# Where the small work stands in an attention and MLP block: splits, heads' pieces, the last steps and two sums

## The chip, the cores and the metric

The kernel runs on one core of a Trainium2 chip. The metric is the device time of one execution in microseconds, lower is better; several executions are timed and their median is taken. Engines are named as the profile names them: PE (matrix products; PEld its weight loads), DVE, ACT, POOL, and SP, which here issues every DMA. Each engine works through its instructions in the order in which the program lists them, and waits where an input isn't there yet.

## The reference

One transformer block with adaptive layer norm, 2048 tokens of width 512, 32 heads of width 16, an MLP of width 1792 with mish, all in float32.

```python
mod = (_silu(c) @ w_mod).reshape(c.shape[0], 6, 1, -1)
sa, ca, ga, sb, cb, gb = (mod[:, 0], mod[:, 1], mod[:, 2], mod[:, 3], mod[:, 4], mod[:, 5])
h = _layernorm(x, axis=-1) * (1 + ca) + sa
x = x + ga * _A_ref(h, A_wqkv, A_wo)          # softmax attention over all heads
h = _layernorm(x, axis=-1) * (1 + cb) + sb
x = x + gb * _B_ref(h, B_w1, B_b1, B_w2)      # up (1792) + mish + down (512)
return x
```

where the attention's part is

```python
scores = jnp.einsum("bhqd,bhkd->bhqk", q, k) * scale
p = _softmax(scores, axis=-1)
o = jnp.einsum("bhqk,bhkd->bhqd", p, v)
```

and mish(h) = h tanh(log(1 + e^h)).

## The kernel before

**Steps.** The attention runs over 4 blocks of 512 queries, here called quarters (`qb`), with 8 groups of 4 heads in each (`g`; `n` counts the 32 groups through), and 16 chunks of 128 keys in each group. That makes T = 512 steps `t` of one chunk for one group. A step multiplies scores for its chunk (`score`, L507, four products that use one half of PE's rows), turns them to exponentials on ACT (L515), and adds the weighted values of two steps earlier (`pv`, L535, eight records in the profile). PRO = 20 steps ahead of the scores, the maxima of the scores of later groups are computed (`max_tile`, product L471, reduction on DVE L473). A group's negated maxima are put in place once a group (`max_rows`, L487 to L496: a transpose, two DVE operations, four DMAs `qa<-mt`), in the fourth step before the group begins; the product of the scores subtracts them. In the last 20 steps there are no maxima left to compute.

**Half-steps and hooks.** Everything else is hung between these products. `at(h, f)` lists the function f to be called at half-step h; step t calls the hooks of 2t at its start and those of 2t+1 in its middle. Hooks of one half-step run in the order in which they were listed. A quarter has 256 half-steps, a group 32. `step` writes the order out: what a hook issues is queued on its engine behind all that was issued earlier.

**Units beside the attention.** `queue` holds units: projections of q, k and v in the first quarter, and afterwards, for the query block that the attention has finished, the output projection (`wo_unit`), 14 up units (`up_unit(f)`, 12 products) and 20 down units (`down_unit`, 6 or 12 products). `next_part`, called every second step, cuts the next piece of a unit: all of its products if there are 8 or fewer left, else half of them, so 6 of 12. Each product of a piece is done in two halves, over the lower and over the upper 64 rows (`mm_half`), one in each of the two steps, beside a score or a maximum's product that takes the other half of the rows. A piece of k products gives k halves to each of two steps. Each half is followed by a product of the attention; the first half of the next step waits for the exponential (or the reduction) that reads the product issued right behind the last half (`after`), because both halves add up in one bank. In the last 20 steps a step with f halves spreads its four scores over f slots; with no halves it does two scores at a time.

**Mish.** When an up unit f ends at half-step h (`fin`), its mish is hung at offsets from h, one stage each: clamp (POOL, L735), exponential (ACT, L741), product (POOL, two operations, L749 and L750), logarithm (ACT, L753), inverse (ACT, L756), quotient (POOL, five operations, L765 to L769), place (no instruction), split (POOL, L95 writes `a_h`, L98 writes `a_l`). `done["a", f]` says when a down unit that reads f may begin. In the last part (`idle(h)`) the bias is added on DVE rather than on ACT. While f = 0 to 4 an up unit ends every 8 half-steps; from f = 5 on a down unit stands between, and it is 12 (later 16).

**Heads.** When a group's weighted sums are complete, `evac` copies them to `ot` and hangs up, from `2 * t1`, two half-steps behind the boundary of the group: `sums` (a DMA of the denominators), `rows` (four DMAs `od<-ot`, L564), the reciprocal and its way to `rb`. Every second group, three POOL operations multiply by `rb` (L579) and split the result into `o_hl` (L95, L98). `od` is one buffer for two groups: the rows of the next pair may be written only when the last of these three has read it.

**Modulation and weights.** In the first quarter the other eight half rows of `w_mod` are loaded (`mod_load`), multiplied and added up on POOL (`sums`, L618 to L620), and summed over the partitions by PE (`mod_unit`). These are `specials`: `do_specials` runs at most one a step, at its end; later the same queue holds the transposes of the normed rows. Each modulation sum starts the load of the one two places on; the last one starts `start_preps`, which splits all the weights of the MLP and the output projection (32 `prep_unit`s) and writes them back to HBM.

**The end.** The last query block has no attention left to stand beside. `tail_loads`, at half-step 2T - 30, loads weights for it: `wos`, and `w1s` for f = 0 to 3. Of these f = 2 and 3 go to the two buffers that also serve the last up units. `tail` then does the output projection of this block, the ten down units that were held back (`held`), the layer norm and the MLP. Between the last step and `tail` a loop runs what is still hung up.

Of the kernel before, what the change touches and what calls it, by code (L numbers as in the profile page):

```python
# [18 lines left out]
def adaln_block(ctx: ExitStack, tc: tile.TileContext, x, wqkv, wo, w1, b1, w2, c, w_mod, out):  # L19
# [9 lines left out]
    NB = S // TB  # L29
# [3 lines left out]
    T = 16 * NIT  # L33
# [5 lines left out]
    PRO = 16 + LEAD  # L39
# [46 lines left out]
    def dap(t, off, ap):  # L86
        return bass.AP(tensor=t.tensor, offset=t.offset + off, ap=ap)

    def hi_copy(eng, hi, src):
        if eng == "a":  # L90
            nc.scalar.copy(hi, src)
        elif eng == "v":
            nc.vector.tensor_copy(hi, src)
        else:
            nc.gpsimd.tensor_scalar(hi, src, 1.0, 0.0, op0=ALU.mult, op1=ALU.add)  # L95

    def lo_sub(eng, lo, src, hi):
        (nc.gpsimd if eng == "p" else nc.vector).tensor_sub(lo, src, hi.bitcast(F32))  # L98
# [25 lines left out]
    def mm_go(m):  # L124
        acc, l, r, start, stop = m
        nc.tensor.matmul(acc, l, r, start=start, stop=stop)  # L126
# [11 lines left out]
    def pe_run():  # L138
        while pe_queue:
            mm_go(pe_queue.pop(0))  # L140
# [13 lines left out]
    def bank(tag="ms"):  # L154
        return ring() if tag == "ring" else ps.tile([P, TB], F32, tag=tag, name="bk", bufs=1)
# [29 lines left out]
    def at(h, f):  # L185

        hooks.setdefault(h, []).append(f)
# [122 lines left out]
    with ExitStack() as es:  # L310
# [107 lines left out]
        for tb in range(NB):  # L418
# [5 lines left out]
            for kind in (1, 0) if tb == 0 else (1,):  # L424
                fin = qk_unit(kind, 0, tb, "ring")
# [117 lines left out]
    def evac(n):  # L543
        qb, g = divmod(n, G)
        t1 = 16 * (n + 1) + 1
        if g == 0:
            o_hl[qb] = [ap.tile([P, DK, TB], F32R, tag=f"o_{i}", name="o_hl", bufs=1) for i in range(2)]
        ot = ap.tile([P, TB], F32, tag="ot", name="ot", bufs=1)
        nc.scalar.copy(ot, accs.pop(n))
        if g % 2 == 0:  # L550
            st["od"] = ap.tile([P, TB], F32, tag="od", name="od", bufs=1)
            st["rb"] = ap.tile([P, TB], F32, tag="rb", name="rb", bufs=1)
        od, rb = st["od"], st["rb"]
        b = 64 * (g % 2)
        if n == NIT - 1:
            mst["last"] = (ot, od, rb)
            return
        sm = ap.tile([P, 16], F32, tag="sm", name="sm", bufs=2)
        def sums():
            nc.sync.dma_start(sm, ot[DH::32, :])  # L560

        def rows():
            for h in range(4):
                nc.sync.dma_start(od[b + 16 * h:b + 16 * h + 16, :], ot[32 * h:32 * h + DH, :])  # L564

        rc = ap.tile([P, 16], F32, tag="rc", name="rc", bufs=2)
        hurry = g == G - 1
        at(2 * t1 + 2, sums)
        at(2 * t1 + (12 if g == 2 else 3), rows)
        at(2 * t1 + (5 if hurry else 12), lambda: nc.vector.reciprocal(rc, sm))  # L570
        at(2 * t1 + (6 if hurry else 13), lambda: nc.sync.dma_start(rscr[n], rc))
        at(2 * t1 + (8 if hurry else 17),
           lambda: nc.sync.dma_start(rb[b:b + 64, :], dap(rscr, n * 4 * TB, [[TB, 4], [0, DH], [1, TB]])))
        if g % 2 == 1 or n == NIT - 2:
            r = slice(0, P if g % 2 else 64)

            oh, ol = o_hl[qb]
            k, d = 2 * t1 + (36 if g == 1 else 11 if hurry else 23), 0 if hurry else 2
            at(k, lambda: nc.gpsimd.tensor_mul(od[r], od[r], rb[r]))  # L579
            at(k + d, lambda: hi_copy("p", oh[r, g // 2, :], od[r]))  # L580
            at(k + 2 * d, lambda: lo_sub("p", ol[r, g // 2, :], od[r], oh[r, g // 2, :]))
# [85 lines left out]
    def load_w1(f):  # L667
        return load_split("w1", 2, w1scr[f])
# [42 lines left out]
    def up_mms(acc, w, hh, hl):  # L711
        mm3(acc, [w1v(w, 0, k) for k in range(DK)], [w1v(w, 1, k) for k in range(DK)],
            [hh[:, k, :] for k in range(DK)], [hl[:, k, :] for k in range(DK)], "b")
# [67 lines left out]
    def idle(h):  # L781

        return h is not None and 2 * (T - PRO) + 2 < h <= 2 * T
# [5 lines left out]
    def block(qb, t0):  # L789

        xn, y, act, w1s, w2s, wos, done, hx = {}, {}, {}, {}, {}, {}, {}, []
# [58 lines left out]
        def up_unit(f, tag):  # L850
            w = w1s.pop(f)
            acc = bank(tag)
            up_mms(acc, w, *hx)
            act[f], (bias, *stages) = mish(f, acc, False)

            def fin(h):
                bias(idle(h))
                for i, s in zip((1, 3, 4, 9, 13, 13 if f < 4 else 14, 16, 18) if f < 5 else (1, 5, 6, 9, 13, 14, 16, 18), stages):
                    at(h + i, s)
                done["a", f] = h + 20  # L860
                if f + 2 < FT:
                    w1s[f + 2] = load_w1(f + 2)
                elif qb + 1 < len(blocks):
                    blocks[qb + 1]["w1"][f + 2 - FT] = load_w1(f + 2 - FT)
            return fin
# [95 lines left out]
    def half_tile(t, j, scr):  # L961

        w = t[:, j * 2 * D:(j + 1) * 2 * D]
        nc.sync.dma_start(w.bitcast(F32), scr.rearrange("p v m -> p (v m)"))
        return w.rearrange("p (v m) -> p v m", v=2)

    def w1_tail(f):
        i, j = divmod(f % 8, 2)
        return load_w1(f) if i == 1 else half_tile(ka[(1, 0, 2, 3)[i]], j, w1scr[f])

    def tail_loads():
        for k in range(DK):
            wos[k] = half_tile(ka[(4, 0)[k // 2]], k % 2, woscr[k])
        for f in range(4):
            w1s[f] = w1_tail(f)

    def tail():
# [4 lines left out]
        for i in range(4):  # L982
            r = 4 * last + i
            nc.sync.dma_start(y[i], x[r * P:(r + 1) * P, :])
        for f in range(4, 8):
            w1s[f] = w1_tail(f)
        accs4 = [bank("ms"), bank("acc")] + [None, None]

# [51 lines left out]
        act, stages = {}, {}  # L1040
        LAG = 4
        for u in range(FT + LAG):
# [11 lines left out]
            f = u - LAG  # L1054
            if f >= 0:
                a_h, a_l = act.pop(f)
                w = w2s.pop(f)
                for i in range(4):
                    s = slice(i * P, (i + 1) * P)
# [14 lines left out]
    units, specials = [], []  # L1074
# [9 lines left out]
    def next_part(h):  # L1084

        if not cur["left"] and units and h >= units[0][0]():
            cur["h"] = h
            cur["fin"] = units.pop(0)[1]("ms")
            cur["left"], cur["first"] = list(pe_queue), True
            cur.pop("after", None)  # L1090
            pe_queue.clear()
        slots = []
        for m in cur["left"]:
            if slots and len(slots[-1]) < 2 and m[0].shape[-1] <= TB // 2:
                slots[-1].append(m)
            else:
                slots.append([m])
        n = len(slots)
        k = n if n <= 8 else (n + 1) // 2
        cur["part"], cur["left"] = slots[:k], [m for l in slots[k:] for m in l]  # L1100

    def whole_units(h, credit):
# [24 lines left out]
    def step(t):  # L1127
# [23 lines left out]
        if not second and 1 < t < T:  # L1151
            next_part(2 * t)
# [67 lines left out]
            f()  # L1220

    def do_specials(h):
        if specials and h >= specials[0][0]():
            fin = specials.pop(0)[1]()
            pe_run()
            at(h + 1, lambda: fin(h + 1))


    plan = [(-PRO, 2, 0, range(4, 16)), (-PRO, 1, 1, range(NB)), (-PRO, 0, 1, (0,)), (-PRO, 1, 2, range(NB)),
# [128 lines left out]
```

## Time and profile before

| what | us |
|---|---|
| runs: median (lowest, highest) | 1726.91 (1724.11, 1729.96) |
| the profiled execution | 1725.0 |
| its span | 1723.2 |
| busy: PE / DVE / ACT / POOL | 1677.6 / 1427.8 / 1341.0 / 887.3 |
| L471, products for maxima, 2048 | 782.1 |
| L507, products for scores, 2048 | 719.9 |
| L535, weighted sums, 4096 records | 547.2 |
| L473, reductions on DVE, 2048 | 1278.4 |
| L515, exponentials on ACT, 2048 | 1089.0 |

In a row of a timeline the first number is the start in us from the start of the span, the second the duration (of all that the row merges; x4 means four instructions), then engine, line, operation, what it writes <- what it reads, and the shape; in brackets, if the engine was idle before it, for how long and what ended that. A row of the waits has the waiting engine and line, what it waited for, and us in total, the number of waits, the longest. Matmuls overlap on PE, so their durations add up to more than the time; the distance between starts is what counts.

### The profile page before, as it was taken

Reading aid. Unit: us, or ns where it says so; the run is one execution under the profiler, and the core shown is the slowest. Engines: PE = TensorE matmul, PEld = TensorE weight load, DVE = VectorE, ACT = ScalarE, POOL = GpSimd, SP = SyncE. Lnnn points to the kernel's source line nnn. Section 1 sums busy time; section 2 is a strip of 40 time slices with the busy share of each in tenths; the row PEclk is TensorE's granted clock in tenths of the full one; section 3 lists DMA queues with packets and bytes.
Section 4 is the critical chain, followed back from the end, with each engine's and each line's share of the span. In section 5 each row is a group of like instructions: output and inputs, shape, how many; then the busy total and the mean of one; then the engine's idle time right before and its main releaser. Section 6 shows DMA issues by size and latency. Waiting matters only on the chain.

```text
span 1723.2 us, 32800 instructions
## 1 busy us (share of the span) xinstructions
PE 1677.6 (97%) x12236; PEld 930.9 (54%) x12236; DVE 1427.8 (83%) x2352; ACT 1341.0 (78%) x2605; POOL 887.3 (51%) x868
## 2 busy tenths in 40 slices
PE   7999999999999999999999999999999999999998
PEld 5755655455435454555555554555555545553676
DVE  6888888888898888888888888888888888880467
ACT  6257777777779898888889898888888888888364
POOL 5155224565403297755524496655433687636542
PEclk9999999999999999999999999999999999999999
DMA  7677456777763333435342644344343534332261
GB/s 239 186 226 220 113 175 196 241 231 218 224 201 86 104 101 84 119 77 154 101 111 64 195 104 101 92 130 117 97 110 97 163 82 115 92 105 105 98 228 65
DMA packets 113993, 240.03 MB, mean 139 GB/s; under 512 B 24049, under 2 KB 49649, under 8 KB 107785
## 3 DMA queue, kind: packets, MB, share of 16 engines
q1 hardware_dynamic: 113832, 237.92, 48.8%
q8 instruction: 97, 1.59, 0.4%
q14 instruction: 64, 0.52, 0.1%
HBM read 179.95 MB, written 51.44 MB: 134 GB/s over the span
## 4 chain that ended last, share of the span: by engine, by line
PE 82%; POOL 6%; DMA 5%; ACT 3%; DVE 2%; issue 1%; SPq 1%; ACTq 0%; DVEq 0%; POOLq 0%
PE bk L535 26%; PE ring L471 21%; PE ring L507 19%; PE bk L132 8%; PE bk L126 3%; PE ring L126 2%; ACT pr L515 2%; DMA qscr<-ql 1%; PE ring L1061 1%; DMA w2scr<-hl 1%; POOL y L880 1%; POOL a_l L98 1%; DMA ka<-kscr 1%; DMA wma<-in_w_mod 1%; DVE mx L473 1%
## 5 line engine op out<-in xcount | busy, mean ns | idle before, releaser
L473 DVE TENSOR_REDUCE mx<-ring 128x1 f32<-128x512 f32 x2048 | 1278.4, 684 | 180.3 <-PE bk L132 122.6
L515 ACT ACTIVATE pr<-ring 128x512 f32<-128x512 f32 x2048 | 1089.0, 611 | 235.4 <-PE bk L132 153.1
L471 PE MATMUL ring<-ka,qa 64*128 64x512 f32 x2048 | 782.1, 427 | 8.3 <-ACT pr L515 7.4
L507 PE MATMUL ring<-qa,ka 64*128 64x512 f32 x2048 | 719.9, 398 | 11.5 <-DMA qa<-mt 6.8
L471 PEld LDWEIGHTS ring<-ka,qa 64*128 64x128 f32 x2048 | 366.9, 184 | 421.8 <-DVE mx L473 355.3
L535 PE MATMUL bk<-pr,vg 128*32 128x512 f32 x4096 | 547.2, 606 | 0.0
L507 PEld LDWEIGHTS ring<-qa,ka 64*128 64x128 f32 x2048 | 373.4, 185 | 115.6 <-ACT pr L515 47.8
L132 PE MATMUL bk<-h,w 64*128 64x512 f32 x1008 | 283.1, 412 | 1.5 <-ACT pr L515 1.5
L132 PE MATMUL bk<-w,a_h 64*128 64x512 f32 x576 | 194.0, 416 | 0.5 <-ACT pr L515 0.5
L132 PEld LDWEIGHTS bk<-h,w 64*128 64x128 f32 x1008 | 172.5, 185 | 11.2 <-ACT pr L515 4.4
L535 PEld LDWEIGHTS bk<-pr,vg 128*32 128x32 f32 x4096 | 81.2, 108 | 126.2 <-issue 118.7
L735 POOL TENSOR_SCALAR ee<-hb 128x512 f32<-128x512 f32 x42 | 62.4, 1486 | 102.5 <-ACT hb L729 100.5
L765 POOL TENSOR_TENSOR ee<-ee,rr 128x512 f32<-128x512 f32 x42 | 53.8, 1280 | 117.0 <-ACT rr L756 116.8
L132 PE MATMUL bk<-w,a_l 64*128 64x512 f32 x288 | 113.5, 394 | 0.0
L132 PEld LDWEIGHTS bk<-w,a_h 64*128 64x128 f32 x576 | 95.6, 185 | 9.2 <-ACT pr L515 3.3
L880 POOL TENSOR_TENSOR y<-yd,y 128x512 f32<-128x512 f32 x50 | 64.2, 1284 | 45.9 <-ACT yd L879 44.9
L132 PE MATMUL bk<-w,o_hl 64*128 64x512 f32 x288 | 79.6, 409 | 0.0
L98 POOL TENSOR_TENSOR a_l<-hb,a_h 128x512 fp32r<-128x512 f32 x53 | 71.7, 1352 | 4.4
L753 ACT ACTIVATE rr<-ee,two 128x512 f32<-128x512 f32 x56 | 40.6, 726 | 21.4 <-POOL ee L750 12.7
L132 PE MATMUL bk<-h_h,wl 64*128 64x512 f32 x168 | 57.0, 422 | 0.0
L750 POOL TENSOR_TENSOR ee<-ee,rr 128x512 f32<-128x512 f32 x42 | 54.1, 1288 | 3.5
L769 POOL TENSOR_TENSOR hb<-hb,rr 128x512 f32<-128x512 f32 x42 | 54.2, 1289 | 3.3
(204 smaller groups left out, 1805.5 us busy)
## 6 DMA issues: line engine op xcount, KB each, us to landing
ka<-kscr SPq DMA_DIRECT2D x124, 384.0 KB
w<-w2scr SPq DMA_DIRECT2D x56, 512.0 KB
w<-w1scr SPq DMA_DIRECT2D x46, 512.0 KB
vg<-vscr SPq DMA_DIRECT2D x32, 552.0 KB
qa<-qscr SPq DMA_DIRECT2D x124, 100.0 KB
kscr<-qh SPq DMA_DIRECT2D x16, 512.0 KB
qscr<-qh SPq DMA_DIRECT2D x32, 256.0 KB
hl<-in_B_w SPq DMA_DIRECT2D x28, 256.0 KB
```

Source lines behind the costliest of these rows:

```text
L98: (nc.gpsimd if eng == "p" else nc.vector).tensor_sub(lo, src, hi.bitcast(F32))
L126: nc.tensor.matmul(acc, l, r, start=start, stop=stop)
L132: i = nc.tensor.matmul(acc, l[64 * g:64 * g + 64], r[64 * g:64 * g + 64], start=start, stop=stop)
L471: nc.tensor.matmul(pm, qt[64 * s:64 * s + 64, qs * P:(qs + 1) * P], kt[64 * s:64 * s + 64, kb * TB:(kb + 1) * TB], start=True, stop=True)
L473: return nc.vector.tensor_reduce(out=mxs[n][:, s, 4 * j + qs, kb:kb + 1], in_=pm, op=ALU.max, axis=AX.X)
L507: nc.tensor.matmul(p_, kt[64 * s:64 * s + 64, kc * P:(kc + 1) * P], qt[64 * s:64 * s + 64, :], start=True, stop=True)
L515: e = nc.scalar.activation(pr, p_, AF.Exp, scale=SCALE)
L535: nc.tensor.matmul(accs[n][32 * h:32 * h + 32, :], vgs[n][:, o:o + 32], pts.pop((t, h)), start=(kc == 0), stop=(kc == 15))
L735: nc.gpsimd.tensor_scalar_min(buf("ee", 2), b["hb"], HCAP)
L750: nc.gpsimd.tensor_mul(ee, ee, rr)
L769: nc.gpsimd.tensor_mul(hb, hb, rr)
L880: nc.gpsimd.tensor_add(y[i], yd, y[i])
```

## The change

Four things.

- In `up_unit` the stages of f = 4 and later keep their places but for the split, which goes from 18 to 19, and `done` from 20 to 21 (`late`). For f = 4 the quotient was at 14 already.
- In `evac` the three POOL operations of a quarter's second group (g = 1) go from 36, 38, 40 to 42, 46, 50; for the other groups but the last of a quarter the distance between them goes from 2 to 4. The rows of the third group (g = 2) go from 12 to 24.
- In `next_part` a piece has 3 products from half-step 2(T - PRO) on, that is in the last 20 steps; `tail_loads` loads two blocks of w1 instead of four, and `tail` the others.
- `do_specials` may run two in a step in the first quarter.

```diff
-        at(2 * t1 + (12 if g == 2 else 3), rows)
+        at(2 * t1 + (24 if g == 2 else 3), rows)
...
-            k, d = 2 * t1 + (36 if g == 1 else 11 if hurry else 23), 0 if hurry else 2
+            k, d = 2 * t1 + (42 if g == 1 else 11 if hurry else 23), 0 if hurry else 4
             at(k, lambda: nc.gpsimd.tensor_mul(od[r], od[r], rb[r]))
             at(k + d, lambda: hi_copy("p", oh[r, g // 2, :], od[r]))
             at(k + 2 * d, lambda: lo_sub("p", ol[r, g // 2, :], od[r], oh[r, g // 2, :]))
...
-                for i, s in zip((1, 3, 4, 9, 13, 13 if f < 4 else 14, 16, 18) if f < 5 else (1, 5, 6, 9, 13, 14, 16, 18), stages):
+                late = f >= 4
+                for i, s in zip((1, 3 if f < 5 else 5, 4 if f < 5 else 6, 9, 13, 13 + late, 16, 18 + late), stages):
                     at(h + i, s)
-                done["a", f] = h + 20
+                done["a", f] = h + 20 + late
...
     def tail_loads():
         for k in range(DK):
             wos[k] = half_tile(ka[(4, 0)[k // 2]], k % 2, woscr[k])
-        for f in range(4):
+        for f in range(2):
             w1s[f] = w1_tail(f)
...
-        for f in range(4, 8):
+        for f in range(2, 8):
             w1s[f] = w1_tail(f)
...
         k = n if n <= 8 else (n + 1) // 2
+        if h >= 2 * (T - PRO):
+            k = 3
...
     def do_specials(h):
-        if specials and h >= specials[0][0]():
-            fin = specials.pop(0)[1]()
-            pe_run()
-            at(h + 1, lambda: fin(h + 1))
+        for _ in range(2 if h < 2 * T // NB else 1):
+            if specials and h >= specials[0][0]():
+                fin = specials.pop(0)[1]()
+                pe_run()
+                at(h + 1, lambda fin=fin: fin(h + 1))
```

## The prediction

> **What bounds the kernel now.** I read the chain that ended last first, then the weighted sums (PE line L535, eight records a step) as a ruler for the length of a step, then the stretches where a step is long.
>
> ```profile
> PE 82%; POOL 6%; DMA 5%; ACT 3%; DVE 2%; issue 1%; SPq 1%; ACTq 0%; DVEq 0%; POOLq 0%
> ```
>
> The chain is PE's for 82%, but POOL, which is busy only half the time, holds 6%. A plain step takes 2.84 us (first row below, from one L535 to the next). The other rows, in time order, are the stretches that matter: a long step in each of the last three quarters, what follows the second and third of them, and a slightly long one; the columns are the stretch's length, busy us (and instructions) of PE, PEld, DVE, ACT and POOL, the granted clock, the DMA share and GB/s.
>
> ```profile
> 658.65:661.49 2.84, 2.84 (x25) 1.55 (x23) 2.78 (x6) 1.58 (x4) 2.76 (x4) 1.00 0.13 53
> 661.49:667.35 5.86, 3.38 (x25) 1.54 (x23) 3.27 (x7) 3.26 (x7) 2.39 (x3) 1.00 0.01 3
> ...
> 1035.12:1041.89 6.77, 4.32 (x25) 1.96 (x23) 3.46 (x7) 3.69 (x7) 2.36 (x3) 0.84 0.01 2
> 1041.89:1045.34 3.45, 3.45 (x26) 1.60 (x24) 2.33 (x5) 2.43 (x6) 1.48 (x1) 0.82 0.46 152
> 1410.22:1416.80 6.58, 4.11 (x25) 1.79 (x23) 3.42 (x8) 3.57 (x7) 2.47 (x3) 0.88 0.01 2
> 1416.80:1420.50 3.70, 3.70 (x24) 1.58 (x22) 2.37 (x5) 2.47 (x5) 1.48 (x1) 0.76 0.42 146
> ...
> 681.49:684.65 3.16, 3.16 (x24) 1.46 (x22) 2.67 (x6) 3.11 (x7) 0.02 (x1) 1.00 0.21 44
> ```
>
> The three long steps sit at the same place of their quarter: at the mish of up unit f=5, 8 steps after the heads' pieces of the quarter's second group. The timelines of PE, ACT and POOL show who waits for whom.
>
> ```profile
> 662.49 0.28 PE L487 MATMUL ring<-ident,mm 128*32 128x128 f32 x1
> 665.25 0.50 PE L471 MATMUL ring<-ka,qa 64*128 64x512 f32 x1 [2.48 <-ACT pr L515]
> ...
> 664.00 0.72 ACT L753 ACTIVATE rr<-ee,two 128x512 f32<-128x512 f32 x1 [2.98 <-POOL ee L750]
> ...
> 635.06 1.29 POOL L579 TENSOR_TENSOR od<-od,rb 128x512 f32<-128x512 f32 x1
> ...
> 647.97 1.31 POOL L98 TENSOR_TENSOR o_hl<-od,o_hl 128x512 fp32r<-128x512 f32 x1
> ...
> 660.04 0.62 POOL L95 TENSOR_SCALAR a_h<-hb 128x512 fp32r<-128x512 f32 x1
> 660.75 1.29 POOL L98 TENSOR_TENSOR a_l<-hb,a_h 128x512 fp32r<-128x512 f32 x1
> 662.00 0.62 POOL L749 TENSOR_SCALAR rr<-ee 128x512 f32<-128x512 f32 x1
> 662.70 1.26 POOL L750 TENSOR_TENSOR ee<-ee,rr 128x512 f32<-128x512 f32 x1
> 668.02 1.49 POOL L735 TENSOR_SCALAR ee<-hb 128x512 f32<-128x512 f32 x1 [4.05 <-ACT hb L729]
> ```
>
> POOL has run without a gap since before 635 and is some 5 us late; f=5's product (L749, L750) ends at 663.96; ACT's logarithm waits 2.98 us for it, with the exponentials of the scores queued behind it on ACT; PE then has no score bank left and waits 2.48 us. Right behind, POOL is idle for 4.05 us: the jam is one of order, not of load.
>
> **The split behind the next product (`late`).** For f=4 the split goes from 18 to 19 half-steps behind its unit, f=5's product stays at 6, and the two units end 12 apart (half-steps 356 and 368 in the second quarter): 374 against 374 before (the split was registered first), 375 against 374 after. So a_h and a_l change places with the product. From 660.04 to 662.00 that is 1.96 us, and the product ends at 662.00. ACT then waits 1.0 instead of 2.98, PE about 0.5 instead of 2.48. Nobody waits soon for the split itself: the down units that read f=4 are queued some 30 half-steps later, and its `done` moves by one with it. **Gain 3 x 1.95 = 5.9 us.** At least 0 (if POOL fills the time otherwise), at most the whole waits, 3 x 2.5 = 7.5.
>
> **The clock behind two of the stalls.** In the second and third stall the granted clock falls to 0.82 and 0.76 over the following step. Against the first stall's 5.86 and a plain 2.84, they cost 0.91 + 0.61 and 0.72 + 0.86 more, **3.1 us** together. With stalls of 0.5 us I take all of it as gone; it stays if an equal gap stays (bounds 0 and 3.1). The Trainium skill ("TensorE: Matmul & The Clock Gate", HAM oscillation) warns only of idle gaps over about 3.4 us; by that rule a gap of 2.5 us would not lower the clock, this term would be 0 and the time 1715. Here the rows speak for the gap: the low clock comes right behind it both times, and the other rows show 1.00.
>
> The same order matters for f=6 and f=7, where a small wait shows:
>
> ```profile
> 681.54 0.72 ACT L753 ACTIVATE rr<-ee,two 128x512 f32<-128x512 f32 x1 [0.49 <-POOL ee L750]
> ...
> ACT rr L753 <- POOL ee L750: 12.7, 12, 3.0
> ```
>
> Three of the twelve waits are the 3.0s; the rest is small. A step with one is 3.16 long, 0.32 over a plain one, and I count two such steps in each of three quarters: **1.9 us**, gone when the product stands 1.96 us earlier (bounds 0 and 1.9).
>
> **The heads' pieces further apart.** For the second group the three POOL operations move from 358, 360, 362 to 364, 368, 372: still ahead of f=5's product at 374, so the same 3.2 us stand before it. With POOL never idle there, their order among themselves moves nothing: each operation's input (the yd copy, ACT's exponential and inverse, rb) is there before POOL comes to it. **0**; if POOL did run dry in between, up to 1 us of loss a quarter. For other groups the spread is 4 more half-steps on a POOL that has gaps: 0. The rows' DMA of the third group goes from 14 to 26 half-steps behind the boundary of its group, one half-step ahead of the negated maxima's DMAs on SP. That queue is in order:
>
> ```profile
> 649.30 2.98 SPq L564 DMA_DIRECT2D od<-ot  x4
> ...
> 663.48 2.81 SPq L496 DMA_DIRECT2D qa<-mt  x4
> ...
> SPq L496 <- DVE mx L473: 194.3, 18, 15.7
> ```
>
> Today the rows wait until 649.27 for the heads' last subtraction (od is read until then). Moved, that subtraction ends at about 660.0, the four DMAs take 2.98 us and are issued by 663.0, while the maxima are not there before 663.46: **0**, by half a microsecond; if SP is 3 us later than that, PE waits (rival (e)).
>
> **Three halves a step at the end.** In the last 20 steps no maxima run. Now the first ten take six halves each and the last ten none.
>
> ```profile
> 1549.80:1578.31 28.51, 26.47 (x182) 12.01 (x182) 3.42 (x7) 23.14 (x46) 16.47 (x16) 1.00 0.34 130
> 1578.31:1598.69 20.38, 20.38 (x121) 6.48 (x120) 1.00 (x2) 19.87 (x43) 14.03 (x13) 1.00 0.15 40
> ...
> 1573.88 0.38 PE L132 MATMUL bk<-h,w 64*128 64x512 f32 x1
> 1574.10 0.40 PE L132 MATMUL bk<-h,w 64*128 64x512 f32 x1
> ...
> 1576.71 0.50 PE L132 MATMUL bk<-h,w 64*128 64x512 f32 x1 [0.51 <-ACT pr L515]
> ...
> 1578.31 1.07 PE L535 MATMUL bk<-pr,vg 128*32 128x512 f32 x8
> ...
> 1579.96 1.06 PE L535 MATMUL bk<-pr,vg 128*32 128x512 f32 x8
> ...
> 1575.06 0.63 ACT L756 ACTIVATE rr<-rr 128x512 f32<-128x512 f32 x1
> 1575.58 1.08 ACT L515 ACTIVATE pr<-ring 128x512 f32<-128x512 f32 x2
> ...
> 1593.90 7.25 ACT L515 ACTIVATE pr<-ring 128x512 f32<-128x512 f32 x14
> ```
>
> 48.9 us in all. In the first part ACT is busy 23.1 of 28.5 us, and yet PE waits for it: the first half of a step waits for the exponential of the score beside the last half of the step before (`after`), here the one that ends at 1576.66. So any further ACT operation lengthens a step. In the second part ACT is busy throughout. A step of two slots takes 1.65 (1578.31 to 1579.96), and pairs start 0.22 to 0.23 us apart, so six slots make 2.57 and four (four scores, three with a half beside them) 2.12. PE's slots are 80 before and 80 after; what is to be gained is overlap with ACT. ACT has 80 exponentials of 0.518 (7.25 over 14), 2.07 a step, and five other operations instead of eight, since f=13's three fall behind the end, each 0.52 (1575.06 to 1575.58) to 0.6. The halves now wait for the third exponential of a step, not the fourth, so for 0.52 less than with six slots, and PE's own 2.12 decides. 20 x 2.14 + 5 x 0.55 = 45.6, **3.3 less**. The last exponentials lag a little less. I take **3.5**; bounds: ACT alone, 80 x 0.518 + 2.75 = 44.2, gains 4.7; steps as long as with six slots, 20 x 2.57, lose 2.5.
>
> f=13's mish now runs behind the last weighted sum, where POOL was idle until the tail's layer norm:
>
> ```profile
> 1602.28 0.59 ACT L549 COPY ot<-bk 128x512 f32<-128x512 f32 x1 [1.14 <-PE bk L535]
> ...
> 1615.34 0.19 POOL L106 TENSOR_SCALAR ln_rs<-ln_mv 128x1 f32<-128x1 f32 x1 [11.09 <-DVE ln_mv L105]
> ...
> 1575.83 1.28 POOL L765 TENSOR_TENSOR ee<-ee,rr 128x512 f32<-128x512 f32 x1 [7.04 <-ACT rr L756]
> ...
> 1584.13 1.28 POOL L98 TENSOR_TENSOR a_l<-hb,a_h 128x512 fp32r<-128x512 f32 x1
> ```
>
> Behind the copy at 1602.87 come the exponential (0.62), the product (1.96), logarithm and inverse (1.35), then quotient and split, 1575.83 to 1585.41 less a clamp between them (1.49, row at 668.02), 8.1: 12 us and some handing over, to about 1615, just as the layer norm asks for POOL. **A loss of 0.5**, between 0 and 2. SP is freed of a long wait by `range(2)`; what waited behind it has slack, 0, and the two later loads are needed only some 45 us on.
>
> **Two sums in one step.**
>
> ```profile
> 124.84 0.72 POOL L620 TENSOR_TENSOR wm<-wm 128x256 f32<-128x256 f32 x1
> ...
> 124.47 0.67 PE L126 MATMUL ring<-wm,ones 128*128 128x256 f32 x2
> ```
>
> The second sum of the first pair is ready at 125.56 and would now be asked for at 125.0: 0.5 us lost. Each pair saves one switch of PE's tiling, some 0.13: **0**, within 0.7. The weight preparations start two half-steps earlier and end one slot earlier, but the first block's units wait for their own time: 0, within 3 either way, because the first quarter's SP queue is re-timed.
>
> **The sum:** 5.9 + 3.1 + 1.9 + 3.5 - 0.5 = 13.9 less. The profiled execution took 1725.0 (its span 1723.2), the median of the runs is 1.9 above it; 1725.0 - 13.9 = 1711.1, raised by half of that difference, is **1712**.
>
> **Rivals.**
> (a) The jam goes wholly, and the stage reaches ACT's bound: 7.5 + about 1 for the slow starts, 3.1, 1.9 and 4.7 are 18.2: **1708**. For it: POOL's 4.05 us idle right behind. Against: the heads still stand ahead of the product.
> (b) The change doesn't reach the jam: POOL is as late as before when the product's turn comes, the waits stay long enough for the low clock, and only the stage and half of the small waits count: **1722**.
> (c) The stage gives nothing, since ACT's extra operations lengthen every coupled step: **1715 to 1718**.
> (d) The low clock has a cause of its own and stays, 3.1 less gained: **1715**. For it speaks the first stall, 2.48 us at a clock of 1.00 behind it; against it, that both low clocks begin within the long step. The Trainium skill's rule above would have it so.
> (e) Slower. SP: the rows and the re-timed preparations get ahead of the maxima's DMAs, and PE waits at the group boundaries. That happens today at one boundary:
>
> ```profile
> PE ring L507 <- DMA qa<-mt: 2.6, 1, 2.6
> ```
>
> If all seven boundaries of the first quarter and the three later ones with moved rows paid that, 26 less the 2.6 paid now, and half of them the clock's 1.5, it would be 31 more: **1743**. It decides once SP reaches the maxima's DMAs some 3 us late. Against: SP was idle waiting for the maxima themselves at 18 boundaries in the row above.
>
> **Chances.** Forecast 0.48, (a) 0.15, (b) 0.12, (c) 0.13, (d) 0.04, (e) 0.08. No change means within 0.3%, 5.2 us, about what a measurement here can tell. Faster: the forecast, (a), (c), (d) and half of (b), 0.86; same 0.06; slower 0.08. From (a) with the first quarter's 3 below it, to (b): 1704 to 1722.
>
> **What would show it.** Right: the three long steps fall to about 3.5 us, no low clock behind them, the logarithm's waits for POOL fall from 12.7 to about 3; the last 20 steps take about 45.5 us at an even 2.15 to 2.7 each; POOL's first layer norm operation is late by under 1 us. Wrong: a low clock in the second half, waits of PE for qa<-mt at more boundaries than now, or a gap on PE in the tail.

## The result, and the profile after

The changed kernel takes 1706.22 us (median of 4 runs, 1705.84 to 1711.86). The kernel before, run on the same chip, takes 1728.07 (4 runs, 1724.11 to 1729.96). The ratio is 0.9889, with a 95% interval of 0.9866 to 0.9911: faster by about 1.1%. The prediction was 1712 within 1704 to 1722, so the direction and the range held, and the time is 5.8 us below the forecast. The two profiled executions are 1725.0 and 1705.9, with spans of 1723.2 and 1704.1; the 19.1 us between the spans are what the rows below account for.

The first line of the chain of waits of the changed kernel, to be held against the one of before:

```profile
PE 85%; POOL 6%; ACT 3%; DMA 3%; DVE 1%; issue 1%; SPq 1%; DVEq 0%; ACTq 0%; POOLq 0%
```

PE's share is up by 3 points and the DMAs' share down by 2. POOL keeps its 6%, so the chain alone would not show that three stalls behind POOL have become small. The stretches between weighted sums show it. In the same places as before, for the changed kernel (columns: length, busy us and instructions of PE, PEld, DVE, ACT, POOL, then granted clock, DMA share, GB/s):

```profile
659.94:663.90 3.96, 3.38 (x25) 1.52 (x23) 3.27 (x7) 3.25 (x7) 2.43 (x3) 1.00 0.13 30
663.90:666.74 2.84, 2.84 (x25) 1.52 (x23) 2.50 (x5) 2.64 (x7) 1.49 (x1) 1.00 0.29 72
1031.04:1035.00 3.96, 3.38 (x25) 1.52 (x23) 3.28 (x7) 3.27 (x7) 2.42 (x3) 1.00 0.13 29
1402.14:1406.17 4.03, 3.38 (x26) 1.53 (x24) 3.29 (x7) 3.26 (x7) 2.49 (x3) 1.00 0.13 30
678.09:680.91 2.82, 2.82 (x24) 1.51 (x22) 2.47 (x5) 2.65 (x7) 0.00 (x0) 1.00 0.22 45
1537.42:1560.00 22.58, 22.05 (x153) 8.77 (x152) 3.09 (x7) 21.83 (x45) 12.81 (x12) 1.00 0.43 154
1560.00:1581.47 21.47, 21.41 (x153) 8.95 (x151) 0.77 (x2) 21.08 (x43) 11.98 (x11) 1.00 0.00 1
```

The three long steps are 3.96, 3.96 and 4.03 instead of 5.86, 6.77 and 6.58, all at the full clock, and so is what follows them. The step of f=6 has lost its small wait (2.82, it was 3.16). The last 20 steps, in two halves of ten, take 44.05 instead of 48.9.

The timeline of POOL and then of ACT and PE around the first long step of the changed kernel shows the exchange itself:

```profile
657.27 1.29 POOL L98 TENSOR_TENSOR o_hl<-od,o_hl 128x512 fp32r<-128x512 f32 x1
658.51 0.63 POOL L749 TENSOR_SCALAR rr<-ee 128x512 f32<-128x512 f32 x1
659.23 1.28 POOL L750 TENSOR_TENSOR ee<-ee,rr 128x512 f32<-128x512 f32 x1
660.48 0.62 POOL L95 TENSOR_SCALAR a_h<-hb 128x512 fp32r<-128x512 f32 x1
661.18 1.27 POOL L98 TENSOR_TENSOR a_l<-hb,a_h 128x512 fp32r<-128x512 f32 x1
...
660.54 0.72 ACT L753 ACTIVATE rr<-ee,two 128x512 f32<-128x512 f32 x1 [1.08 <-POOL ee L750]
...
661.80 0.50 PE L471 MATMUL ring<-ka,qa 64*128 64x512 f32 x1 [0.58 <-ACT pr L515]
```

Before, a_h and a_l stood ahead of L749 and L750; now they stand behind. The product ends at 660.51, the logarithm waits 1.08 us (it was 2.98) and PE 0.58 (it was 2.48).

The views of the waits over the whole execution put it in two rows. Of the changed kernel:

```profile
ACT rr L753 <- POOL ee L750: 5.4, 4, 2.1
PE ring L471 <- ACT pr L515: 1.8, 3, 0.6
```

and of the kernel before, the second of them:

```profile
PE ring L471 <- ACT pr L515: 7.4, 3, 2.5
```

The same three waits of PE, 7.4 us, are 1.8 us now. The longest of ACT's four, 2.1, is f=13's own mish behind the last step and not one of the three.

**Where the 19.1 us are.** From the start of each kernel's first long step back to the start of the span the changed execution is 1.55 us ahead (661.49 against 659.94). The three long steps, each with the step behind it, gave 8.7 (before 5.86 + 2.84, 6.77 + 3.45 and 6.58 + 3.70; now 6.8 to 6.9 each). The six small waits gave 1.9. The last 20 steps gave 4.9. The end of the last weighted sums gave 0.8. The tail up to the last group of output DMAs gave nothing, and the landing of the last DMA gave 1.1.

### The profile page after: what moved, and what is told of

Read it like the earlier page. It is cut to its first block, busy times and chain, and to the rows that moved or that the text cites. A ratio compares the mean times of both kernels' runs of the same rounds, so it can differ in the third digit from the quotient of the medians.

```text
span 1704.1 us, 32797 instructions
## 1 busy us (share of the span) xinstructions
PE 1667.8 (98%) x12236; PEld 929.6 (55%) x12236; DVE 1427.7 (84%) x2352; ACT 1342.4 (79%) x2605; POOL 889.5 (52%) x868
## 3 DMA queue, kind: packets, MB, share of 16 engines
q1 hardware_dynamic: 113832, 237.92, 48.9%
## 4 chain that ended last, share of the span: by engine, by line
PE 85%; POOL 6%; ACT 3%; DMA 3%; DVE 1%; issue 1%; SPq 1%; DVEq 0%; ACTq 0%; POOLq 0%
PE bk L535 27%; PE ring L471 22%; PE ring L507 20%; PE bk L132 8%; PE bk L126 3%; PE ring L126 2%; ACT pr L515 2%; PE ring L1062 1%; DMA qa<-mt 1%; DMA wr<-in_A_wqkv 1%; POOL y L881 1%; DMA wm<-in_w_mod 1%; POOL rr L767 1%; POOL ee L765 1%; POOL hb L768 1%
## 5 line engine op out<-in xcount | busy, mean ns | idle before, releaser
L749 POOL TENSOR_SCALAR rr<-ee 128x512 f32<-128x512 f32 x42 | 26.1, 622 | 59.8 <-ACT ee L741 59.7
L750 POOL TENSOR_TENSOR ee<-ee,rr 128x512 f32<-128x512 f32 x42 | 54.1, 1288 | 3.5
```

## The experiments

The kernel before was run again with each group of kernels; its medians were 1724.88 (25 runs), 1726.35 (13) and 1726.05 (13). Ratios below are against the runs of their own group.

### One part at a time, on the kernel before

**The split alone** (`late`, nothing else):

```diff
+                late = f >= 4
+                for i, s in zip((1, 3 if f < 5 else 5, 4 if f < 5 else 6, 9, 13, 13 + late, 16, 18 + late), stages):
...
+                done["a", f] = h + 20 + late
```

> Only the split of f = 4 and later one half-step later. Theory: it alone empties the jam, since the product of f=5 changes places with the split of f=4. The three long steps 5.9, 6.8 and 6.6 fall to about 4.0, no low clock behind them, the steps of 3.16 go to 2.84: 8.7 + 1.9 = 10.6 us less, about 1714.5 in an execution of 1725. Rival: the heads' pieces had to move too; then the long steps stay over 5 and the time within 3 us of before.

Measured: 1713.62 us (4 runs), ratio 0.9929 [0.9911, 0.9948]. The stretch of its first long step, columns as above:

```profile
659.66:663.56 3.90, 3.38 (x26) 1.53 (x24) 3.29 (x7) 3.26 (x7) 2.36 (x3) 1.00 0.00 1
```

The other two are 3.87 and 3.91, at a clock of 1.00 as well. One exchange of two pairs of POOL operations shortens all three, and removes the low clock and the small waits, with the heads' pieces where they were. The last 20 steps stay at 48.98.

**Three halves a step alone:**

```diff
-        for f in range(4):
+        for f in range(2):
...
-        for f in range(4, 8):
+        for f in range(2, 8):
...
+        if h >= 2 * (T - PRO):
+            k = 3
```

> Only three halves a step in the last 20 steps, and the two loads of w1 in the tail. Theory: the 20 steps fall from 49.0 to 44.0 us, the last weighted sums end 0.8 earlier behind them, the tail is not longer for f=13's mish: 5.7 us less, about 1719.3. Rival: part of the 5 us came from the stretch before (the phase of PE and ACT that the jam leaves); then the 20 steps stay over 46.

Measured: 1719.92 us (10 runs), ratio 0.9972 [0.9961, 0.9982]. The 20 steps take 44.05, exactly as in the changed kernel. The long steps are still there (6.69, 6.60 and 6.44), and here the low clock comes at all three.

**The heads' pieces and the rows alone:**

```diff
-        at(2 * t1 + (12 if g == 2 else 3), rows)
+        at(2 * t1 + (24 if g == 2 else 3), rows)
...
-            k, d = 2 * t1 + (36 if g == 1 else 11 if hurry else 23), 0 if hurry else 2
+            k, d = 2 * t1 + (42 if g == 1 else 11 if hurry else 23), 0 if hurry else 4
```

> Only the heads' pieces further apart and the third group's rows later. Theory: nothing in the last three quarters, since the three operations still stand ahead of f=5's product: the long steps stay at 5.9 to 6.8, the time within 2 us of before, and what differs lies in the first quarter. Rival: the heads carry the gain; then the long steps fall by 3 us each or more and the time by 9.

Measured: 1725.22 us (10 runs), ratio 0.9996 [0.9985, 1.0008]: nothing. The long steps are 7.06, 6.97 and 6.76, with the low clock at all three. In the waits of this kernel the stall of PE is where it was:

```profile
PE ring L471 <- ACT pr L515: 7.3, 3, 2.4
```

**Two sums in one step alone** (`do_specials`):

```diff
+        for _ in range(2 if h < 2 * T // NB else 1):
+            if specials and h >= specials[0][0]():
...
+                at(h + 1, lambda fin=fin: fin(h + 1))
```

> Only two modulation sums in one step in the first quarter. Theory: the steps with a sum lose 0.3 us in all, and the preparations that start two half-steps earlier move the waits for qa<-mt at three boundaries (5.7, 4.9, 4.4 before; 4.3, 4.0, 7.0 in the changed kernel): the first quarter's time is within 2 us of before and so is the whole. Rival: the first quarter owes its difference to the heads' rows in front of qa<-mt; then these three steps stay as before here, and change in the run with the heads alone.

Measured: 1724.51 us (10 runs), ratio 0.9993 [0.998, 1.0005]: nothing. In the timeline of PE in the changed kernel, the second sum of the first pair, and both sums of the second pair in one row:

```profile
125.74 0.70 PE L126 MATMUL ring<-wm,ones 128*128 128x256 f32 x2 [0.72 <-POOL wm L620]
...
146.70 1.10 PE L126 MATMUL ring<-wm,ones 128*128 128x256 f32 x4 [0.18 <-DVE mx L473]
```

The first pair asks for its second sum 0.72 us before POOL has it; from weighted sums to weighted sums, its two steps take 7.81 instead of 7.12, 0.69 lost. The second pair's inputs are there, both sums go through together, and its two steps take 7.18 instead of 7.47. The ten steps that hold both pairs take 32.0 in the changed kernel as in the one before, but that needs 0.4 from a step between them which was longer before, and such a longer step comes and goes in executions with and without this edit. In the run with the sums alone PE waits 1.4 us for the first pair's second sum, and its two steps take 8.49; the time of the whole doesn't show it.

The four ratios multiply to 0.9890.

**The changed kernel again:**

> The changed kernel itself, beside the next three. The parts one by one gave 11.3, 5.0, -0.3 and 0.4 less; if they add up, it is 16.4 less than before, 1708.5, and if they help each other in the first quarter it is nearer to 1706.

Measured: 1706.1 us (4 runs, 1705.49 to 1707.5), ratio 0.9886 [0.9867, 0.9906]. As ratios the parts add up to the whole (0.9890 and 0.9886). As medians they give 16.4 us and the whole 20.2 below the kernel before of its own group; the parts ran in another group, so whether they help each other by a few us is not shown.

### One part taken out of the changed kernel

**Without the split behind the product:**

```diff
-                late = f >= 4
...
-                done["a", f] = h + 20 + late
+                done["a", f] = h + 20
```

> The changed kernel with the split and done of f = 4 and later put back. Theory: the jam is back whole, though the heads' pieces stand further apart: three steps of 5.9 to 7.1 us and the steps of 3.16, 11 us more than the changed kernel. Rival: with the heads moved the split matters less; then under 6 us more.

Measured: 1719.2 us (10 runs), ratio 0.9961 [0.9945, 0.9977], 13.1 us above the changed kernel of the same group. The stretches of its first two long steps (the third is 6.94, at a clock of 0.82):

```profile
662.22:668.13 5.91, 3.38 (x25) 1.53 (x23) 3.28 (x7) 3.25 (x7) 2.44 (x3) 1.00 0.10 22
1036.09:1043.17 7.08, 4.59 (x25) 2.25 (x24) 3.47 (x7) 3.69 (x7) 2.40 (x3) 0.81 0.08 18
```

The jam is back at its full size although the heads' pieces are further apart, with the low clock within two of the three.

**Without the heads' pieces and rows** (the two lines of `evac` as they were):

```diff
-        at(2 * t1 + (24 if g == 2 else 3), rows)
+        at(2 * t1 + (12 if g == 2 else 3), rows)
...
-            k, d = 2 * t1 + (42 if g == 1 else 11 if hurry else 23), 0 if hurry else 4
+            k, d = 2 * t1 + (36 if g == 1 else 11 if hurry else 23), 0 if hurry else 2
```

> The changed kernel with the heads' pieces and the rows put back. Theory: the same three steps of 3.9 us and the same time within 1.5 us, since the three operations stand ahead of f=5's product either way. Rival: the move keeps SP from waiting 15 us for the heads' last subtraction, and that is worth something in the loads behind it; then over 2 us more.

Measured: 1707.76 us (4 runs), ratio 0.989 [0.9861, 0.9918]. The long steps are 3.96, 3.97 and 3.94. The median is 1.7 us above the changed kernel of the same group, a little more than the 1.5 of the theory, but the intervals cover each other. With the split moved or not moved, the heads' pieces as the change places them do nothing that these runs can tell.

### What is left at the jam

In the changed kernel the last of the heads' pieces, `lo_sub` at half-step 372 (657.27 in POOL's timeline above), still stands ahead of f=5's product at 374. If order is all that matters, it has to go behind the product too, and the rows behind it.

```diff
-            at(k + 2 * d, lambda: lo_sub("p", ol[r, g // 2, :], od[r], oh[r, g // 2, :]))
+            at(k + (12 if g == 1 else 2 * d), lambda: lo_sub("p", ol[r, g // 2, :], od[r], oh[r, g // 2, :]))
...
-        at(2 * t1 + (24 if g == 2 else 3), rows)
+        at(2 * t1 + (28 if g == 2 else 3), rows)
```

> The changed kernel with the second group's last subtraction behind f=5's product (from 50 to 54) and the third group's rows behind the maxima's DMAs (from 24 to 28). Theory: what is left of the wait, 0.9 us in each of the three steps, goes with the 1.3 us that no longer stand before the product: the steps fall from 3.96 to 3.1 us, 2.6 us less than the changed kernel. Rival: the rows, now later, keep the next copy of ot on ACT waiting, and the steps behind the group's boundary get longer by as much.

Measured: 1703.12 us (4 runs), ratio 0.987 [0.985, 0.989], 3.0 below the changed kernel of the same group, though the two intervals overlap. In its timeline of POOL, and in the stretch of what was the first long step, the reason can be read:

```profile
656.91 1.28 POOL L750 TENSOR_TENSOR ee<-ee,rr 128x512 f32<-128x512 f32 x1
...
660.10 1.29 POOL L98 TENSOR_TENSOR o_hl<-od,o_hl 128x512 fp32r<-128x512 f32 x1
```

```profile
658.86:661.91 3.05, 3.05 (x25) 1.50 (x24) 2.87 (x6) 2.67 (x7) 2.53 (x2) 1.00 0.00 0
```

The product now ends at 658.19, the heads' subtraction follows, and PE is busy for all 3.05 us of the step: nothing of the stall is left. All three are 3.05 long. Three times 0.91 less is 2.7 of the 3.0 us. The rival isn't there: in the view of the waits of this kernel, ACT's copy of `ot` waits for PE and for ACT's own exponentials, and for no DMA. So the forecast's sentence that the heads' pieces move nothing as long as all of them stand ahead of the product fits the runs, and the useful question was which of them have to stand there.

### The boundaries of groups in the first quarter

With the jam gone, the longest single waits left on PE during the attention are those for `qa<-mt`. Three late boundaries of the first quarter in the kernel just above (in the changed kernel these steps take 4.27, 4.01 and 6.95):

```profile
337.06:341.99 4.93, 3.15 (x24) 1.49 (x22) 2.73 (x5) 2.60 (x7) 3.19 (x4) 0.99 0.72 199
386.65:389.49 2.84, 2.84 (x24) 1.48 (x22) 2.48 (x5) 2.55 (x7) 2.67 (x3) 1.00 0.79 186
432.25:440.08 7.83, 4.27 (x25) 2.10 (x23) 2.84 (x5) 3.16 (x7) 4.26 (x5) 0.83 0.71 181
```

Two kernels, both built on this one, try two ways to bring these DMAs earlier. The first issues them on ACT's queue for the first quarter:

```diff
-                    nc.sync.dma_start(
+                    (nc.scalar if n < G else nc.sync).dma_start(
```

> The kernel of the run before (last piece behind the product), with the four DMAs of the negated maxima issued from ACT instead of SP for the groups of the first quarter. Theory: the long steps at three boundaries of the first quarter (4.9, 2.9, 7.8 there, 2.83 without a wait) come from what stands ahead of these DMAs on SP; they go to 2.9 each, the low clock behind them goes too, and with it the scatter: 5 us less, about 1698. Rival: the DMA engines are busy there (0.7 of their time), so the transfer itself is late; then the steps stay over 3.5.

Measured: 1723.46 us (10 runs), ratio 0.9982 [0.9966, 0.9998], some 20 us worse than without it. Two rows of the waits of this kernel, and one of its stretches ahead of a boundary (the like ones at the two boundaries before it are 7.77 and 7.45 long):

```profile
ACT pr L515 <- DMA qa<-mt: 14.3, 4, 5.3
PE ring L507 <- DMA qa<-mt: 0.5, 1, 0.5
```

```profile
446.10:454.48 8.38, 4.41 (x24) 2.13 (x23) 2.98 (x6) 3.16 (x6) 3.88 (x5) 0.78 0.58 198
```

PE's wait for the DMAs is almost gone (0.5), but ACT now stands for up to 5.3 us at a time before its next exponential, and PE runs out of score banks as it did at the jam, with the low clock too.

The second leaves the queue and moves what stands ahead of these DMAs on it, the weight preparations that fall on half-step 22 of a group:

```diff
         then = clear(max(h + PREP, puts[0] + 1 if len(puts) > 2 - (not three) else 0))
+        if 130 < then < 220 and then % 32 == 22:
+            then += 12
```

> The same kernel of the run before, with the weight preparation that starts 10 half-steps ahead of a boundary (150, 182, 214) put off behind it. Theory: the queue on SP ahead of the maxima's DMAs is shorter by a load and a put, and the three steps fall to below 4 us each: 2 to 4 us less. Rival: SP is late for what it waits for (puts that must land), not for its count of DMAs; then the three steps stay, and the end of the preparations at half-step 246 costs nothing either.

Measured: 1697.03 us (4 runs, 1696.13 to 1700.41), ratio 0.984 [0.9813, 0.9866], the best of all kernels here. Its stretches at the same three boundaries:

```profile
338.45:342.57 4.12, 3.11 (x25) 1.48 (x23) 2.67 (x5) 2.56 (x7) 2.97 (x3) 1.00 0.83 200
385.78:388.62 2.84, 2.84 (x25) 1.49 (x23) 2.49 (x5) 2.56 (x7) 1.91 (x2) 1.00 0.83 190
431.42:434.25 2.83, 2.83 (x25) 1.53 (x23) 2.48 (x5) 2.55 (x7) 2.18 (x3) 1.00 0.74 178
```

They take 9.8 us together, against 15.6 above. SP's timeline ahead of the third boundary, in the kernel above:

```profile
428.55 0.34 SPq L648 DMA_DIRECT2D hl<-in_B_w  x1
...
430.09 4.54 SPq L496 DMA_DIRECT2D qa<-mt  x4
```

and with the preparation put off:

```profile
425.27 4.42 SPq L496 DMA_DIRECT2D qa<-mt  x4
```

At this boundary the four DMAs are issued 6.2 us ahead of the step (431.42) instead of 2.2 (432.25), while the DMA share during their issue is no lower (0.78 against 0.68): here the place in SP's order counted, not the load. The load of `hl` itself starts only after SP has stood still for 1.4 us, so the rival's waiting of SP has a part in what goes away. At the first boundary the four are issued 4.7 us ahead instead of 3.2, and the step still takes 4.12, so more than the place counts there. At the second there was no wait in the kernel above either. Between the first of these steps and the end of the third the two executions differ by 7.2 us; 5.0 of them are the third step and 2.3 the first with the step behind it. Such boundaries also differ from one execution to the next (the first takes 4.27 and 6.60 in two executions of the changed kernel), and the two kernels, 1703.12 and 1697.03, ran in different groups with intervals that overlap a little, so how much of the 6 us between their medians would come back each time stays open.

### The last 20 steps: four halves a step

```diff
-            k = 3
+            k = 4
```

> The changed kernel with four halves a step in the last 20 steps. Theory: three is right because the first half of a step then waits for the third exponential of the step before; with four it waits for the fourth, and steps of 2.12 become 2.6, as with six: the 20 steps take 48 to 52 us instead of 44.1, 4 to 8 us more. Rival: only PE's slots count, which are 72 here instead of 80; then they take 44 or less.

Measured: 1709.27 us (4 runs), ratio 0.9908 [0.9883, 0.9932]. The stretches of its 20 steps, in two halves:

```profile
1536.05:1560.75 24.70, 23.08 (x159) 9.13 (x157) 2.82 (x6) 22.60 (x46) 12.76 (x12) 1.00 0.37 135
1560.75:1582.60 21.85, 21.31 (x145) 7.94 (x144) 1.60 (x3) 19.40 (x40) 12.22 (x11) 1.00 0.02 7
```

46.55 us, 2.5 more than with three, but less than the 48 to 52 expected; the rival, 44 or less, falls too. In all but two of the first sixteen steps, a step of some 2.1 to 2.2 us alternates with one of 2.6 to 3.2. A piece gives its halves to two steps, and the first half of the second step is the one that waits for an exponential of the first; between one piece and the next nothing waits. So the wait falls on every second step only, where the working had it on every step.

## Why the prediction was right, point by point

**The jam is one of order** (term 5.9). Right in mechanism and nearly in size. The logarithm was to wait 1.0 and PE 0.5; they wait 1.08 and 0.58. The split alone does it, taking the split out brings the jam back, and moving the last head piece behind the product as well removes the rest. Rival (b), a change that doesn't reach the jam, falls with the long steps of 3.96. Among the signs, "about 3.5 us" for these steps was too low by the forecast's own sum, 5.86 - 1.95 = 3.9.

**The clock behind the stalls** (term 3.1). Right. With the term above it makes 9.0, and the long steps and their successors gave 8.7. In five profiled executions with stalls of about 2.5 us (before, the three kernels with another part alone, the changed kernel without the split) the low clock came at 12 of 15 stalls; in the five with the split moved and stalls of 0.5 to 0.65 us left, at none of 15. Rival (d) falls. That the term fits so closely is in part luck: two of three stalls had the low clock in the execution it was read from, all three in others (the last section shows on what that hangs). The rule that the prediction weighed, from the Trainium skill ("TensorE: Matmul & The Clock Gate", HAM oscillation), which warns of gaps over about 3.4 us, is no safe limit here: these gaps were 2.4 to 2.6 us.

**The small waits** (1.9). Right: six steps of some 3.15 are steps of 2.84 or less.

**The heads' pieces and the rows' DMA** (0 and 0). Right: 0.9996 alone, and no loss when taken out. SP's timeline in the changed kernel shows the margin that was put at half a microsecond:

```profile
658.58 2.48 SPq L564 DMA_DIRECT2D od<-ot  x4
661.94 2.83 SPq L496 DMA_DIRECT2D qa<-mt  x4
```

The rows are issued by 661.06 and SP stands idle for 0.9 us before the maxima are there. Rival (e) doesn't decide. But its price was misread: the row with one wait of 2.6 us was asked for the stretch around a single boundary. Over the whole execution PE waits for these DMAs at five places before (first row) and at four after:

```profile
PE ring L507 <- DMA qa<-mt: 6.8, 5, 2.6
...
PE ring L507 <- DMA qa<-mt: 4.8, 4, 2.6
```

With 6.8 instead of 2.6 paid already, that rival would have come out some 4 us lower.

**Three halves a step** (3.5). The mechanism was right, the term was too small. It measured 4.9, and 0.8 more from the end of the last weighted sums, which was within the same term ("the last exponentials lag a little less"). The step that failed is the sum 20 x 2.14 + 5 x 0.55 = 45.6, in which each of ACT's other operations was added in full to PE's steps. Sixteen of the twenty steps take 2.12 or a little less, and the other four, where these five operations fall, take 2.45, 2.78, 2.54 and 2.45: 1.7 us more in all, not 2.75. The forecast's other bound, ACT alone, 80 x 0.518 + 2.75 = 44.2, is near the measured 44.05; but PE is busy for 43.5 of these 44.05 us and ACT for 42.9, so the runs don't tell which of the two sets the pace. The two loads of w1 that moved to the tail were not run apart from the three halves. The exponentials of the changed kernel run on behind one another, and the last weighted sums end sooner behind them:

```profile
1563.02 9.36 ACT L515 ACTIVATE pr<-ring 128x512 f32<-128x512 f32 x18
...
1581.47 2.78 PE L535 MATMUL bk<-pr,vg 128*32 128x512 f32 x24
```

Before, the last row was

```profile
1598.69 3.55 PE L535 MATMUL bk<-pr,vg 128*32 128x512 f32 x24
```

A likely reason for 1.7 instead of 2.75 is that ACT's four exponentials take 2.07 a step and PE's 2.12, so ACT comes to such an operation with a little in hand, and that only every second step waits for ACT at all (the run with four halves); no run isolates it. Rival (c) falls with 44.05 against 48.9.

**Rival (a)**, 1708, is nearer to the measured time than the forecast, but half of its mechanism isn't there: the stage came out at ACT's bound as it says (44.05 against 44.2), while the jam didn't go wholly, since a wait of 0.58 us is left on PE at each of the three places. It goes wholly only where the last head piece is moved too, in a kernel that takes 1703.

**f=13's mish ahead of the layer norm** (-0.5). It costs nothing. POOL in the changed kernel:

```profile
1597.73 0.19 POOL L106 TENSOR_SCALAR ln_rs<-ln_mv 128x1 f32<-128x1 f32 x1
...
1603.84 1.29 POOL L881 TENSOR_TENSOR y<-yd,y 128x512 f32<-128x512 f32 x1
```

and in the kernel before the last of these:

```profile
1621.82 1.29 POOL L880 TENSOR_TENSOR y<-yd,y 128x512 f32<-128x512 f32 x1
```

The collision is there as worked out: the first operation of the layer norm starts 13.5 us behind the end of the weighted sums (1584.25 to 1597.73), where it was 13.1 (1602.24 to 1615.34). But the sum with the residual starts 19.6 us behind that end in both. The layer norm has four such operations one after another, the later ones each waiting for DVE; the second starts 14.6 us behind the end in both kernels, so a late first one is made up.

**Two sums in one step** (0). Right for the whole time (0.9993). The bound of 0.7 on the first pair holds in the changed kernel's execution (0.69 lost, 0.29 gained on the second pair), while other executions with this edit lose up to 1.7 there.

**The preparations.** The step "start two half-steps earlier and end one slot earlier" was half wrong: in the order of the program the first six begin at half-steps 58 to 86 instead of 60 to 84, and from the seventh (99) on both kernels have the same slots. It was costed at 0, and nothing hung on the mistake.

**What no term covered.** The 1.55 us in the first quarter and the 1.1 us in the landing of the last DMA. The last group of output DMAs is issued 114.3 us behind the end of the weighted sums in both kernels (before first, then after):

```profile
1716.49 2.42 SPq L1067 DMA_DIRECT2D out<-pr  x4
...
1698.55 2.43 SPq L1068 DMA_DIRECT2D out<-pr  x4
```

and the span ends 6.7 us after the first and 5.6 us after the second. No edit touches that, and it is scatter: the runs with the heads' pieces alone and with the sums alone, whose tail is that of the kernel before, end 5.6 us after it, and the split alone 6.7. In the first quarter the boundaries of groups differ between executions of one kernel as much as between the kernels. The half of 1.9 us that was added for the way from a profiled execution to the median was too much for the same reason: the changed kernel's median is 0.3 above its profiled execution. So of the 5.8 us by which the forecast was short, some 2.2 are the last 20 steps and the end of the sums, 0.5 the mish, and the rest is of this kind, within what executions of one kernel differ by.

## What to carry to other kernels

An engine that is busy half the time can still hold the critical path where its list is saturated for a few microseconds; then look which of its operations somebody waits for soon, and move those that nobody waits for behind it, rather than spreading them over the stretch. Ask of a stall on the matrix engine also what the clock does behind it, since here a gap of 2.5 us cost up to 1.6 us more. Where two engines run a stage at nearly the same rate, don't add one's extras in full to the other's sum: here five operations of about 0.55 us on ACT lengthened the stage by 1.7 us. Work out both sums and give them as bounds.

## What the hardware showed that was not expected

**The clock after a short gap.** In the run with three halves alone, the granted clock in the 3.4 us that begin within the first long step (0.50 and 0.51 within the others), and the waits that go with all three:

```profile
664.30:667.70 3.40, 3.40 (x20) 1.37 (x16) 2.27 (x4) 2.85 (x5) 0.90 (x1) 0.50 0.17 42
```

```profile
PE ring L471 <- ACT pr L515: 7.3, 3, 2.5
```

The clock is at one half for 3.4 us at a time, after waits of 2.5 us at most. It isn't certain: the same gap left the clock at 1.00 at 3 of 15 places. The traces show most of what decides it. In each execution the low stretches begin at points of a fixed grid of 3.413 us (those of the kernel before, at 1039.73 and 1415.20, are 110 such steps apart). The stretches of this grid at the first two stalls of the kernel before:

```profile
660.86:664.27 3.41, 1.91 (x15) 0.58 (x13) 2.43 (x6) 0.43 (x2) 3.02 (x3) 1.00 0.00 0
664.27:667.68 3.41, 2.43 (x18) 1.45 (x22) 1.80 (x3) 3.31 (x7) 0.00 (x0) 1.00 0.02 5
1036.32:1039.73 3.41, 0.96 (x7) 0.48 (x6) 0.95 (x3) 2.13 (x4) 1.24 (x1) 1.00 0.01 2
1039.73:1043.14 3.41, 3.41 (x20) 1.43 (x16) 2.33 (x4) 2.80 (x6) 0.79 (x1) 0.50 0.18 41
```

The first stall lies across a point of the grid, PE is idle for 1.50 us of one stretch and 0.98 of the next, and the clock stays up. The second lies within one stretch, PE is idle for 2.45 of its 3.41 us, and the next one runs at half the clock. Over all 13 profiled executions, from 120 us on and without the last 8 us, every one of the 24 stretches at the full clock with 1.77 us or more of idle PE was followed by one at half. Of those with less than 1.6 us, nearly 6000, one was (0.85 idle, in the run with ACT's queue), and of the five between, one. In the first 120 us, before the steps are regular, it isn't as simple: six low stretches there follow 0.8 to 1.1 us of idle PE. Beyond that, what counts in these runs is PE's idle time within one stretch of the grid, and a gap of 2.5 us is hit or spared by where it falls on it.

**DMA issues on a busy engine.** Four DMAs issued from ACT held it for up to 5.3 us, as the waits of that kernel show above. In the rows of SP shown here the same four take 2.8 to 4.5 us of the queue, and there only other DMAs stand behind them.
